# Turning the value product of a sliding-window attention round: V stationary in four column tiles, weights moving, transposes on VectorE

## The chip, the cores and the metric

The kernel runs on one core of one Trainium2 chip. The metric is the device time of one execution in microseconds (us). Before the change it is 310.59 us (median of 3 runs, 309.92 to 311.50).

Engine names: PE is TensorE's matmul, PEld its weight load, DVE is VectorE, ACT ScalarE, POOL GpSimd, SP SyncE. L233 is line 233 of the kernel of the run in question; the same statement has another line number in another kernel. A matmul has a stationary operand (`lhsT`), which a weight load brings into the array (3260 loads for 3200 matmuls in the kernel before), and a moving operand (`rhs`), whose columns the matmul goes through (512 of them every 0.216 us in this kernel). PSUM is the memory that matmuls write.

## The reference, cut to what matters

```python
# x: 2048 tokens x 512; H = 32 heads of 16; window W = 256; F = 1792; all bf16
xn = layernorm(x)
def attention(xn):
    q, k, v = heads(xn @ wqkv)
    s = q @ k.T * 16 ** -0.5
    s = where((i - j >= 0) & (i - j < 256), s, -1e9)
    return merge(softmax(s) @ v) @ wo
def mlp(xn):
    return ((xn @ w_gate) * (xn @ w_up)) @ w_down
return x + attention(xn) + mlp(xn)
```

## The kernel before

Tokens go in four chunks T of 512. A chunk has eight head groups (c, par) of four heads each, and a head group has three steps i, so there are 96 steps. A step computes scores transposed (keys on partitions, queries along the free axis) for up to two key blocks, takes exp on ACT and masks the result P on POOL. The value product for a step comes two steps later (LAG). Between these, PE gets "filler" from one ordered list: projections, gate and up, down, output product.

In PSUM, `S` (128x2048 in float32) has one buffer, the accumulator one, and everything else shares three buffers `M`.

```python
GROUPS = (((-2, 0, 0, 0), (0, 0, 2, 128)),     # key block, first and last query block, column in P
          ((-1, 0, 1, 0), (2, 2, 3, 256)),
          ((1, 1, 3, 0), (3, 3, 3, 384)))
self.ppool = pool("ppool", 5)
self.ps_s = pool("ps_s", 1, space=PSUM); self.ps_a = pool("ps_a", 1, space=PSUM)
self.ps_m = pool("ps_m", 3, space=PSUM)

def scores(self, T, c, par, i):
    S = self.ps_s.tile([128, 4, 512], F32, tag="S", name="S")
    for kb, q0, q1, col in parts:
        for e in range(4):                       # four row tiles: 16 or 32 rows each
            nc.tensor.matmul(S[:, e, col:col + n], lhsT=K[rows, c, ...], rhs=Q[rows, c, ...],
                             tile_position=(32 * e, 0), ...)
    nc.scalar.activation(out=P[:, :, lo:hi], in_=S[:, :, lo:hi], func=ACT.Exp, scale=0.25)
    # ... masks of P on POOL ...

def values(self, T, c, par, i):                  # P is stationary, V moves
    for n, (kb, q, j, e) in enumerate(todo):     # up to 4 (key, query) block pairs x 4 heads
        nc.tensor.matmul(acc[:, q, e, 0:17], lhsT=P[:, e, j:j + 128],
                         rhs=self.V[U][:, v, 8 * c + 2 * e + par, 0:17], ...)
    if i == 2:                                   # column 16 of V is 1: the softmax sum
        nc.vector.reciprocal(out=rz[:], in_=acc[:, :, :, 16])
        nc.vector.tensor_tensor(out=o[:, :, c, :, par, :], in0=acc[:, :, :, 0:16], in1=rz..., op=ALU.mult)

def o_transpose(self, T, c):                     # O: tokens on partitions -> OT: features on partitions
    ps = self.ps_m.tile([128, 4, 128], BF16, tag="M", name="oTp")
    for q in range(4):
        nc.tensor.transpose(ps[:, q, :], self.O[T][:, q, 128 * c:128 * c + 128], self.ident[:])
    nc.vector.tensor_copy(out=self.OT[T][:, c, :], in_=ps...)

# filler: gate, up, projections are pieces of 4 matmuls (128x512), down of 5, 5, 4
for g, s in enumerate(steps):
    fill(-1, g)
    self.scores(*s)
    half = total * (done_w + weight[g] / 2) / sum(weight)
    fill(half, g)
    if g >= LAG:
        self.values(*steps[g - LAG])
        valued = g - LAG
    done_w += weight[g]
    fill(total * done_w / sum(weight), g)
```

The softmax here doesn't subtract the row's maximum and nothing guards it: scores larger than these inputs give would overflow.

Of the kernel before, what the change touches and what calls it, by code (L numbers as in the profile page):

```python
# [7 lines left out]
BF16 = mybir.dt.bfloat16  # L8
F32 = mybir.dt.float32
I32 = mybir.dt.int32  # L10
ACT = mybir.ActivationFunctionType
ALU = mybir.AluOpType
# [10 lines left out]
class Kernel:  # L23
# [24 lines left out]
    def setup(self):  # L48
        nc, const, NT, NF = self.nc, self.const, self.NT, self.NF
        self.x = const.tile([128, NT, 512], BF16, name="x")  # L50
        self.Wqkv = const.tile([128, 4, 1536], BF16, name="Wqkv")
        self.Wo = const.tile([128, 4, 512], BF16, name="Wo")
        self.Wg = const.tile([128, 4, self.F], BF16, name="Wg")
        self.Wu = const.tile([128, 4, self.F], BF16, name="Wu")
        self.Wd = const.tile([128, NF, 512], BF16, name="Wd")
        xv = self.x_d.rearrange("(t p) d -> p t d", p=128)
        wq = self.w_d["qkv"].rearrange("(k p) n -> p k n", p=128)
        wg = self.w_d["g"].rearrange("(k p) n -> p k n", p=128)
        wu = self.w_d["u"].rearrange("(k p) n -> p k n", p=128)
        for t in range(4):  # L60
            nc.sync.dma_start(out=self.x[:, t, :], in_=xv[:, t, :])
        for lo in (1024, 512, 0):
            nc.scalar.dma_start(out=self.Wqkv[:, :, lo:lo + 512], in_=wq[:, :, lo:lo + 512])
        h = self.F // 2
        nc.sync.dma_start(out=self.x[:, 4:8, :], in_=xv[:, 4:8, :])
        for lo in (0, h):
            nc.sync.dma_start(out=self.Wg[:, :, lo:lo + h], in_=wg[:, :, lo:lo + h])
            nc.sync.dma_start(out=self.Wu[:, :, lo:lo + h], in_=wu[:, :, lo:lo + h])
        nc.sync.dma_start(out=self.x[:, 8:NT, :], in_=xv[:, 8:NT, :])
        nc.sync.dma_start(out=self.Wd[:], in_=self.w_d["d"].rearrange("(f p) n -> p f n", p=128))  # L70
        nc.sync.dma_start(out=self.Wo[:], in_=self.w_d["o"].rearrange("(c p) n -> p c n", p=128))

        warm = const.tile([128, 1], F32, name="warm")
        nc.vector.memset(warm[:], 0.0)
        nc.scalar.activation(out=warm[:], in_=warm[:], func=ACT.Exp)
        ident = const.tile([128, 128], BF16, name="ident")
        nc.gpsimd.memset(ident[:], 0.0)
        nc.gpsimd.affine_select(out=ident[:], in_=ident[:], compare_op=ALU.not_equal, fill=1.0,
                                base=0, pattern=[[-1, 128]], channel_multiplier=1)
        self.ident = ident  # L80
        wps = self.ps_a.tile([128, 128], F32, tag="acc", name="wps")
        for _ in range(36):
            nc.tensor.matmul(wps[:], lhsT=ident[:], rhs=ident[:], start=True, stop=True)
        pi = const.tile([128, 1], I32, name="pi")
        nc.gpsimd.iota(pi[:], pattern=[[0, 1]], base=0, channel_multiplier=1)
        podd = const.tile([128, 1], I32, name="podd")
        nc.vector.tensor_scalar(out=podd[:], in0=pi[:], scalar1=4, scalar2=1,
                                op0=ALU.arith_shift_right, op1=ALU.bitwise_and)
        self.odd = const.tile([128, 1], F32, name="odd")
        nc.vector.tensor_copy(out=self.odd[:], in_=podd[:])  # L90
        self.mhalf = const.tile([128, 4], F32, name="mhalf")
        nc.gpsimd.memset(self.mhalf[:], -0.5)
        self.xnT, self.Q, self.hT, self.O, self.OT = {}, {}, {}, {}, {}
        self.K, self.Ko, self.V = {}, {}, {}
        self.strips, self.acc = {}, {}
# [122 lines left out]
                                            fill=0.0, base=0, channel_multiplier=1)  # L218
        self.strips[(T, c, par, i)] = P

    def values(self, T, c, par, i):
        nc = self.nc
        P = self.strips.pop((T, c, par, i))
        if i == 0:
            self.acc[(T, c, par)] = self.ps_a.tile([128, 4, 4, 18], F32, tag="acc", name="acc")
        acc = self.acc[(T, c, par)]
        first = i == 0
        parts = self.parts(T, i)
        todo = [(kb, q, col + 128 * (q - q0), e) for kb, q0, q1, col in parts
                for q in range(q0, q1 + 1) for e in range(4)]  # L230
        for n, (kb, q, j, e) in enumerate(todo):
            U, v = divmod(4 * T + kb, 4)
            nc.tensor.matmul(acc[:, q, e, 0:17], lhsT=P[:, e, j:j + 128],  # L233
                             rhs=self.V[U][:, v, 8 * c + 2 * e + par, 0:17],
                             start=(first and n == 0), stop=(i == 2 and n == len(todo) - 1),
                             skip_group_check=True)
        if i == 2:
            self.acc.pop((T, c, par))
            if (c, par) == (0, 0):
                self.O[T] = self.chunk2.tile([128, 4, 512], BF16, tag="O", name=f"O{T}")  # L240
                self.OT[T] = self.const.tile([128, 4, 512], BF16, tag="OT", name=f"OT{T}")
            rz = self.small.tile([128, 4, 4], F32, tag="rz")
            nc.vector.reciprocal(out=rz[:], in_=acc[:, :, :, 16])  # L243
            o = self.O[T].rearrange("p q (c e two d) -> p q c e two d", c=4, e=4, two=2)
            nc.vector.tensor_tensor(out=o[:, :, c, :, par, :], in0=acc[:, :, :, 0:16],
                                    in1=rz.unsqueeze(3).to_broadcast([128, 4, 4, 16]), op=ALU.mult)

    def o_transpose(self, T, c):
        nc = self.nc
        ps = self.ps_m.tile([128, 4, 128], BF16, tag="M", name="oTp")  # L250
        for q in range(4):
            nc.tensor.transpose(ps[:, q, :], self.O[T][:, q, 128 * c:128 * c + 128], self.ident[:])  # L252
        nc.vector.tensor_copy(out=self.OT[T][:, c, :], in_=ps.rearrange("p q t -> p (q t)"))


    def gate(self, T, f):
# [55 lines left out]
    def fillers(self):  # L312


        out = []
        NCH, NF, NG = self.NCH, self.NF, 24

        def add(cost, f, before=None, after=None):
            out.append((cost, f, before, after))
# [30 lines left out]
            for lo, hi in ((0, 5), (5, 10), (10, NF)):  # L350
                add(hi - lo, lambda lo=lo, hi=hi: self.down(T, b, lo, hi))

        def ot(T, c):
            add(1, lambda: self.o_transpose(T, c), None, NG * T + 6 * c + 5)

        for c in range(1, 4):
            qk(0, c, 6 * c)
        for T in range(NCH):
            if T:
                for c in range(3):  # L360
                    ot(T - 1, c)
                down(T - 1, 0)
                ot(T - 1, 3)
                for b in range(4):
                    if b:
                        down(T - 1, b)
                    add(4, lambda T=T, b=b: self.finish(T - 1, b))
            gu(T, norms(T + 1) if T + 1 < NCH else {})
            if T + 1 < NCH:
                project(T + 1)  # L370
        T = NCH - 1
        down(T, 0)
        for c in range(3):
            ot(T, c)
        for b in range(4):
            if b:
                down(T, b)
            add(3, lambda b=b: self.finish_early(T, b))
        return [(*o, None, None)[:4] for o in out]

    def run(self):
        self.xns, self.stats, self.y0 = {}, {}, {}
        self.setup()
        NCH, NG, LAG = self.NCH, 24, 2
# [12 lines left out]
        nc = self.nc  # L397
# [6 lines left out]
        done_w, spent, n = 0, 0, 0  # L404
        valued = -1

        def fill(upto, group):
            nonlocal spent, n
            while n < len(work):
                cost, f, before, after = work[n]  # L410
                if after is not None and after > valued:
                    break
                if spent + cost / 2 > upto and not any(
                        w[2] is not None and w[2] <= group for w in work[n:]):
                    break
                f()
                spent += cost
                n += 1

        for g, s in enumerate(steps):  # L420
            fill(-1, g)
            self.scores(*s)
            half = total * (done_w + weight[g] / 2) / sum(weight)
            fill(half, g)
            if g >= LAG:
                self.values(*steps[g - LAG])
                valued = g - LAG
            done_w += weight[g]
            fill(total * done_w / sum(weight), g)
        for g in range(len(steps) - LAG, len(steps)):  # L430
            fill(spent + 11, -1)
            self.values(*steps[g])
            valued = g
        fill(10 ** 9, -1)
        assert n == len(work)
        self.o_transpose(NCH - 1, 3)
        for b in range(4):
            self.finish_late(NCH - 1, b)

# [36 lines left out]
```

## Time and profile before

| | before |
|---|---|
| time, median | 310.59 us |
| span of the profiled run | 308.1 us |
| PE busy | 289.0 us, 94% |
| first scores, first scores of chunk 1, last scores | 21.5, 77.2, 291.1 us |

From the page of the kernel before: the line of busy times (share of the span, then instructions), the rows of PE, DVE and granted clock over 40 equal slices in tenths, the chain of waits by engine, and two groups of instructions (busy us, mean ns of one, then idle time before them).

```profile
PE 289.0 (94%) x3200; PEld 144.1 (47%) x3260; DVE 167.2 (54%) x329; ACT 181.6 (59%) x118; POOL 155.3 (50%) x266
...
PE   6569999999999999999999999999999999999992
...
DVE  3237888646531687863722397772842165663324
...
PEclk9999999999999999999999999999999999999999
...
PE 88%; ACT 4%; DMA 3%; issue 2%; DVE 1%; ACTq 0%; DVEq 0%
...
L207 ACT ACTIVATE P<-S 128x2048 bf16<-128x2048 f32 (+2 forms) x96 | 170.0, 1771 | 95.3 <-PE S L199 90.0
...
L233 PEld LDWEIGHTS <-P 128*128 128x128 bf16 x1440 | 49.7, 96 | 21.0 <-issue 0.2
```

PE is the limit. It is busy for 90% or more of every slice from 4 to 39, and the chain that ended last is PE for 88%. The value product needs 1440 loads of a 128-column stationary operand.

The timeline of PE of the kernel before, in chunk 1 (start us, us, engine, line, operation, output<-moving,stationary, shapes, count):

```profile
123.14 0.59 PE L271 MATMUL up<-xnT_754,Wu 128*128 128x512 bf16 x2
123.78 0.35 PE L233 MATMUL acc<-V_164,P 128*128 128x17 bf16 x8
123.99 0.34 PE L233 MATMUL acc<-V_993,P 128*128 128x17 bf16 x8
124.19 0.38 PE L143 MATMUL xTp<-ident,xn 128*128 128x128 bf16 x4
124.41 1.03 PE L262 MATMUL gp<-xnT_754,Wg 128*128 128x512 bf16 x4
125.37 0.29 PE L199 MATMUL S<-Q_990,Ko_163 32*128 32x256 bf16 x4
```

Read starts, not durations: the durations of pipelined matmuls overlap (one of the value matmuls is shown with 170 ns, and the next starts 25 ns after it). Sixteen value matmuls hold PE from 123.78 to 124.19, 25 ns each, for 17 moving columns. Four transposes hold it for 0.22 us.

The waits of PE in the kernel before (total us, times, longest):

```profile
PE S L199 <- ACT P L207: 0.9, 4, 0.4
```

Scores almost never wait for exp to release the one `S` buffer.

### The profile page before, as it was taken

Reading aid. Unit: us, or ns where it says so; the run is one execution under the profiler, and the core shown is the slowest. Engines: PE = TensorE matmul, PEld = TensorE weight load, DVE = VectorE, ACT = ScalarE, POOL = GpSimd, SP = SyncE. Lnnn points to the kernel's source line nnn. Section 1 sums busy time; section 2 is a strip of 40 time slices with the busy share of each in tenths; the row PEclk is TensorE's granted clock in tenths of the full one; section 3 lists DMA queues with packets and bytes.
Section 4 is the critical chain, followed back from the end, with each engine's and each line's share of the span. In section 5 each row is a group of like instructions: output and inputs, shape, how many; then the busy total and the mean of one; then the engine's idle time right before and its main releaser. Section 6 shows DMA issues by size and latency. Waiting matters only on the chain.

```text
span 308.1 us, 7448 instructions
## 1 busy us (share of the span) xinstructions
PE 289.0 (94%) x3200; PEld 144.1 (47%) x3260; DVE 167.2 (54%) x329; ACT 181.6 (59%) x118; POOL 155.3 (50%) x266
## 2 busy tenths in 40 slices
PE   6569999999999999999999999999999999999992
PEld 5334445544544444554544444554454444444550
DVE  3237888646531687863722397772842165663324
ACT  2246666677566576568657565667657566565600
POOL 3115565455555647456555557555455555554520
PEclk9999999999999999999999999999999999999999
DMA  7998000000000000000000000000001000000001
GB/s 238 371 369 284 3 3 1 2 2 0 3 19 34 19 2 0 2 3 0 2 19 19 34 2 3 0 2 2 2 0 37 19 17 3 2 0 2 2 0 68
DMA packets 10512, 12.27 MB, mean 40 GB/s; under 512 B 496, under 2 KB 10480, under 8 KB 10480
## 3 DMA queue, kind: packets, MB, share of 16 engines
q1 hardware_dynamic: 8896, 10.23, 9.8%
q10 hardware_dynamic: 1584, 1.57, 1.6%
q8 instruction: 25, 0.41, 0.6%
q14 instruction: 7, 0.06, 0.1%
HBM read 9.70 MB, written 2.10 MB: 38 GB/s over the span
## 4 chain that ended last, share of the span: by engine, by line
PE 88%; ACT 4%; DMA 3%; issue 2%; DVE 1%; ACTq 0%; DVEq 0%
PE psd L280 16%; PE up L271 16%; PE gp L262 15%; PE acc L233 11%; PE S L199 10%; PE qkp L165 8%; PE psd L285 4%; PE vp L155 4%; ACT P L207 3%; DMA Wqkv<-in_A_wqkv_dram 3%; PE oTp L252 1%; PE xTp L143 1%; PE qkb L181 1%; DMA out_dram<-y 1%; ACT xnT_184 L146 1%
## 5 line engine op out<-in xcount | busy, mean ns | idle before, releaser
L207 ACT ACTIVATE P<-S 128x2048 bf16<-128x2048 f32 (+2 forms) x96 | 170.0, 1771 | 95.3 <-PE S L199 90.0
L212 POOL TENSOR_SCALAR_AFFINE_SELECT P<-P 128x512 bf16<-128x512 bf16 x128 | 81.5, 637 | 70.4 <-ACT P L207 70.2
L216 POOL TENSOR_SCALAR_AFFINE_SELECT P<-P 128x512 bf16<-128x512 bf16 x112 | 71.6, 639 | 56.8 <-ACT P L207 56.8
L233 PEld LDWEIGHTS <-P 128*128 128x128 bf16 x1440 | 49.7, 96 | 21.0 <-issue 0.2
L265 DVE CAST gsb<-gp 128x512 bf16<-128x512 f32 x56 | 38.3, 684 | 13.8 <-PE gp L262 12.6
L271 PEld LDWEIGHTS <-Wu 128*128 128x128 bf16 x224 | 18.2, 97 | 20.7 <-issue 5.0
L262 PEld LDWEIGHTS <-Wg 128*128 128x128 bf16 x224 | 18.4, 97 | 19.7 <-issue 3.9
L243 DVE RECIPROCAL rz<-acc 128x16 f32<-128x16 f32 x32 | 8.0, 251 | 28.8 <-PE acc L233 28.8
L292 DVE TENSOR_TENSOR y<-psd,x 128x512 bf16<-128x512 f32 x12 | 8.3, 691 | 19.7 <-PE psd L285 19.7
L233 PE MATMUL acc<-V_164,P 128*128 128x17 bf16 x384 | 15.6, 170 | 0.2
L233 PE MATMUL acc<-V_993,P 128*128 128x17 bf16 x384 | 15.5, 170 | 0.2
L233 PE MATMUL acc<-V_2172,P 128*128 128x17 bf16 x384 | 15.5, 170 | 0.2
L165 PEld LDWEIGHTS <-Wqkv 128*128 128x128 bf16 x120 | 9.7, 97 | 10.8 <-issue 2.2
L262 PE MATMUL gp<-xnT_1936,Wg 128*128 128x512 bf16 x54 | 14.3, 379 | 0.1
L262 PE MATMUL gp<-xnT_754,Wg 128*128 128x512 bf16 x54 | 14.3, 379 | 0.1
L262 PE MATMUL gp<-xnT_184,Wg 128*128 128x512 bf16 x53 | 14.1, 379 | 0.2
L271 PE MATMUL up<-xnT_184,Wu 128*128 128x512 bf16 x53 | 14.1, 380 | 0.1
L262 PE MATMUL gp<-xnT_3108,Wg 128*128 128x512 bf16 x53 | 14.1, 380 | 0.1
L271 PE MATMUL up<-xnT_3108,Wu 128*128 128x512 bf16 x52 | 13.9, 380 | 0.1
L280 PE MATMUL psd<-Wd,hT_392 128*128 128x512 bf16 x54 | 13.8, 380 | 0.1
L280 PE MATMUL psd<-Wd,hT_1581 128*128 128x512 bf16 x53 | 13.6, 380 | 0.2
L280 PE MATMUL psd<-Wd,hT_2753 128*128 128x512 bf16 x53 | 13.6, 379 | 0.2
(130 smaller groups left out, 378.9 us busy)
## 6 DMA issues: line engine op xcount, KB each, us to landing
out_dram<-y SPq DMA_DIRECT2D x16, 128.0 KB, 1.7
Wg<-in_B_w_gate_dram SPq DMA_DIRECT2D x2, 896.0 KB, 10.0
Wu<-in_B_w_up_dram SPq DMA_DIRECT2D x2, 896.0 KB, 11.4
Wd<-in_B_w_down_dram SPq DMA_DIRECT2D x1, 1792.0 KB, 17.9
Wqkv<-in_A_wqkv_dram ACTq DMA_DIRECT2D x3, 512.0 KB, 6.2
x<-in_A_x_dram SPq DMA_DIRECT2D x1, 1024.0 KB, 15.0
x<-in_A_x_dram SPq DMA_DIRECT2D x4, 128.0 KB, 5.2
x<-in_A_x_dram SPq DMA_DIRECT2D x1, 512.0 KB, 8.2
```

The costliest lines, as they stand in the source:

```text
L155: nc.tensor.matmul(ps[:], lhsT=self.xnT[T][:, k, 128 * b:128 * b + 128], rhs=self.Wqkv[:, k, 1024:1536], start=(k == 0), stop=(k == 3))
L165: nc.tensor.matmul(ps[:], lhsT=self.Wqkv[:, k, lo:lo + 128], rhs=self.xnT[T][:, k, :], start=(k == 0), stop=(k == 3))
L199: nc.tensor.matmul(S[:, e, col:col + n], lhsT=(self.Ko if par else self.K)[U][rows, c, 128 * j:128 * j + 128], rhs=self.Q[T][rows, c, 128 ...
L207: nc.scalar.activation(out=P[:, :, lo:hi], in_=S[:, :, lo:hi], func=ACT.Exp, scale=0.25)
L212: nc.gpsimd.affine_select(out=P[:, :, j:j + 128], in_=P[:, :, j:j + 128], pattern=[[0, 4], [1, 128]], compare_op=ALU.is_ge, fill=0.0, base ...
L216: nc.gpsimd.affine_select(out=P[:, :, j:j + 128], in_=P[:, :, j:j + 128], pattern=[[0, 4], [-1, 128]], compare_op=ALU.is_gt, fill=0.0, bas ...
L233: nc.tensor.matmul(acc[:, q, e, 0:17], lhsT=P[:, e, j:j + 128], rhs=self.V[U][:, v, 8 * c + 2 * e + par, 0:17], start=(first and n == 0), ...
L262: nc.tensor.matmul(ps[:], lhsT=self.Wg[:, k, 128 * f:128 * f + 128], rhs=self.xnT[T][:, k, :], start=(k == 0), stop=(k == 3))
L265: nc.vector.tensor_copy(out=self.gsb[:], in_=ps[:])
L271: nc.tensor.matmul(ps[:], lhsT=self.Wu[:, k, 128 * f:128 * f + 128], rhs=self.xnT[T][:, k, :], start=(k == 0), stop=(k == 3))
L280: nc.tensor.matmul(self.psd[:], lhsT=self.hT[T][:, f, 128 * b:128 * b + 128], rhs=self.Wd[:, f, :], start=(f == 0), stop=False)
L285: self.nc.tensor.matmul(ps[:], lhsT=self.OT[T][:, c, 128 * b:128 * b + 128], rhs=self.Wo[:, c, :], start=first and c == cs[0], stop=(c == ...
```

## The change

Intent: make the small operand stationary. V of one head (128 keys x 17 columns) is loaded into one of four 32-column tiles of the array, the four heads of a group side by side, and P moves with up to 384 columns per matmul. The sums then come out transposed (features on partitions). Two 32x32 block transposes on DVE bring them to the layout that the output product wants: one in float32 before the division, one in bf16 after it. The PE transposes and their PSUM tiles fall away. The value product of all three steps of a head group is issued in one go, right after a scores block.

```diff
-    def values(self, T, c, par, i):
-        ...
-            nc.tensor.matmul(acc[:, q, e, 0:17], lhsT=P[:, e, j:j + 128],
-                             rhs=self.V[U][:, v, 8 * c + 2 * e + par, 0:17], ...)
-        if i == 2:
-            nc.vector.reciprocal(out=rz[:], in_=acc[:, :, :, 16])
-            nc.vector.tensor_tensor(out=o[:, :, c, :, par, :], in0=acc[:, :, :, 0:16], in1=rz..., op=ALU.mult)
-    def o_transpose(self, T, c): ...
+    def values(self, T, c, par):
+        acc = self.accb                       # one accumulator, set to zero once
+        first = True
+        for i in range(3):
+            P = self.strips.pop((T, c, par, i))
+            for kb, q0, q1, col in self.parts(T, i):
+                n, (U, v) = 128 * (q1 - q0 + 1), divmod(4 * T + kb, 4)
+                for e in range(4):
+                    nc.tensor.matmul(acc[32 * e:32 * e + 17, 128 * q0:128 * q0 + n],
+                                     lhsT=self.V[U][:, v, 8 * c + 2 * e + par, 0:17],
+                                     rhs=P[:, e, col:col + n], start=first, stop=(i == 2),
+                                     tile_position=(0, 32 * e), skip_group_check=True)
+                first = False
+        ...
+        nc.vector.transpose(out=at.rearrange("p b r -> p (b r)"), in_=acc[:])
+        nc.vector.reciprocal(out=rz[:], in_=at[:, :, 16])
+        nc.vector.tensor_tensor(out=self.on[:, :, par, :], in0=at[:, :, 0:16], in1=rz..., op=ALU.mult)
+        if par == 1:
+            nc.vector.transpose(out=self.OT[T][:, c, :], in_=self.on.rearrange("p b r d -> p (b r d)"))
@@ run
+        def values(g):
+            if g >= 0 and steps[g][3] == 2:   # only after the third step of a head group
+                self.values(*steps[g][:3]); valued = g
         for g, s in enumerate(steps):
             fill(-1, g)
             self.scores(*s)
-            half = total * (done_w + weight[g] / 2) / sum(weight)
-            fill(half, g)
-            if g >= LAG:
-                self.values(*steps[g - LAG])
-                valued = g - LAG
+            values(g - LAG)
             done_w += weight[g]
             fill(total * done_w / sum(weight), g)
```

Cut: the fillers that called `o_transpose`, the conditions that hold the output product back until its sums exist, and the PSUM tile of the warm-up matmuls.

More of the change, by code (lines that the diff above doesn't have):

```diff
@@ L80, in setup @@
         self.ident = ident
-        wps = self.ps_a.tile([128, 128], F32, tag="acc", name="wps")
+        self.accb = self.ps_a.tile([128, 512], F32, name="accb")
+        nc.vector.memset(self.accb[:], 0.0)
+        wps = self.ps_m.tile([128, 128], F32, tag="M", name="wps")
         for _ in range(36):
@@ L219, in scores @@
         self.strips[(T, c, par, i)] = P
-    def values(self, T, c, par, i):
+    def values(self, T, c, par):
         nc = self.nc
-        P = self.strips.pop((T, c, par, i))
-        if i == 0:
-            self.acc[(T, c, par)] = self.ps_a.tile([128, 4, 4, 18], F32, tag="acc", name="acc")
-        acc = self.acc[(T, c, par)]
-        first = i == 0
-        parts = self.parts(T, i)
-        todo = [(kb, q, col + 128 * (q - q0), e) for kb, q0, q1, col in parts
-                for q in range(q0, q1 + 1) for e in range(4)]
-        for n, (kb, q, j, e) in enumerate(todo):
-            U, v = divmod(4 * T + kb, 4)
-            nc.tensor.matmul(acc[:, q, e, 0:17], lhsT=P[:, e, j:j + 128],
-                             rhs=self.V[U][:, v, 8 * c + 2 * e + par, 0:17],
-                             start=(first and n == 0), stop=(i == 2 and n == len(todo) - 1),
-                             skip_group_check=True)
-        if i == 2:
-            self.acc.pop((T, c, par))
-            if (c, par) == (0, 0):
-                self.O[T] = self.chunk2.tile([128, 4, 512], BF16, tag="O", name=f"O{T}")
-                self.OT[T] = self.const.tile([128, 4, 512], BF16, tag="OT", name=f"OT{T}")
-            rz = self.small.tile([128, 4, 4], F32, tag="rz")
-            nc.vector.reciprocal(out=rz[:], in_=acc[:, :, :, 16])
-            o = self.O[T].rearrange("p q (c e two d) -> p q c e two d", c=4, e=4, two=2)
-            nc.vector.tensor_tensor(out=o[:, :, c, :, par, :], in0=acc[:, :, :, 0:16],
-                                    in1=rz.unsqueeze(3).to_broadcast([128, 4, 4, 16]), op=ALU.mult)
@@ L248, in o_transpose @@
-    def o_transpose(self, T, c):
-        nc = self.nc
-        ps = self.ps_m.tile([128, 4, 128], BF16, tag="M", name="oTp")
-        for q in range(4):
-            nc.tensor.transpose(ps[:, q, :], self.O[T][:, q, 128 * c:128 * c + 128], self.ident[:])
-        nc.vector.tensor_copy(out=self.OT[T][:, c, :], in_=ps.rearrange("p q t -> p (q t)"))
+        acc = self.accb
[10 more added lines that the diff above has]
+                first = False
@@ new lines, in values @@
+        if (c, par) == (0, 0):
+            self.OT[T] = self.chunk2.tile([128, 4, 512], BF16, tag="OT", name=f"OT{T}")
+        if par == 0:
+            self.on = self.work.tile([128, 16, 2, 16], BF16, tag="on", name="on")
+        at = self.work.tile([128, 16, 32], F32, tag="at", name="at")
+        nc.vector.transpose(out=at.rearrange("p b r -> p (b r)"), in_=acc[:])
+        rz = self.small.tile([128, 16], F32, tag="rz")
+        nc.vector.reciprocal(out=rz[:], in_=at[:, :, 16])
+        nc.vector.tensor_tensor(out=self.on[:, :, par, :], in0=at[:, :, 0:16],
+                                in1=rz.unsqueeze(2).to_broadcast([128, 16, 16]), op=ALU.mult)
@@ L256, in gate @@
+        if par == 1:
+            nc.vector.transpose(out=self.OT[T][:, c, :],
+                                in_=self.on.rearrange("p b r d -> p (b r d)"))
     def gate(self, T, f):
@@ L351, in down @@
                 add(hi - lo, lambda lo=lo, hi=hi: self.down(T, b, lo, hi))
-        def ot(T, c):
-            add(1, lambda: self.o_transpose(T, c), None, NG * T + 6 * c + 5)
         for c in range(1, 4):
@@ L359, in fillers @@
             if T:
-                for c in range(3):
-                    ot(T - 1, c)
                 down(T - 1, 0)
-                ot(T - 1, 3)
                 for b in range(4):
@@ L366, in fillers @@
                         down(T - 1, b)
-                    add(4, lambda T=T, b=b: self.finish(T - 1, b))
+                    add(4, lambda T=T, b=b: self.finish(T - 1, b), None, NG * T - 1)
             gu(T, norms(T + 1) if T + 1 < NCH else {})
@@ L372, in fillers @@
         down(T, 0)
-        for c in range(3):
-            ot(T, c)
         for b in range(4):
@@ L377, in fillers @@
                 down(T, b)
-            add(3, lambda b=b: self.finish_early(T, b))
+            add(3, lambda b=b: self.finish_early(T, b), None, NG * T + 17)
         return [(*o, None, None)[:4] for o in out]
@@ L418, in fill @@
                 n += 1
+        def values(g):
+            nonlocal valued
+            if g >= 0 and steps[g][3] == 2:
+                self.values(*steps[g][:3])
+                valued = g
         for g, s in enumerate(steps):
@@ L422, in run @@
             self.scores(*s)
-            half = total * (done_w + weight[g] / 2) / sum(weight)
-            fill(half, g)
-            if g >= LAG:
-                self.values(*steps[g - LAG])
-                valued = g - LAG
+            values(g - LAG)
             done_w += weight[g]
             fill(total * done_w / sum(weight), g)
-        for g in range(len(steps) - LAG, len(steps)):
-            fill(spent + 11, -1)
-            self.values(*steps[g])
-            valued = g
+        fill(spent + 22, -1)
+        values(len(steps) - 1)
         fill(10 ** 9, -1)
         assert n == len(work)
-        self.o_transpose(NCH - 1, 3)
         for b in range(4):
```

## The prediction

> **What bounds it now.** TensorE. The busy table gives PE 94% of the 308.1 us span (ACT 59%, DVE 54%); the chain of waits is 88% PE. From the first scores (21.5 us) to the last (291 us) the timeline shows almost no PE gap. Costs read from it: a 128x512 matmul every 0.216 us; a block of 16 value matmuls 0.40 us, 25 ns each, although each streams only 17 columns [...]; a scores block 0.42 us with the changes of tiling around it. 888 large matmuls outside prologue and tail (about 194 us), 96 scores blocks (41) and 1440 value matmuls (37) make up the observed 270 us.
>
> **What the change removes from PE.** 1440 value matmuls become 704, moving 128 to 384 columns. Per head group, before: 48 x 25 ns = 1.22 us (0.92 in the first chunk). After: 1536 columns (1152), if the four column tiles run together, 0.64 us (0.48) at the trace's rate, plus about 15 ns per set of four as between the sets of a scores block, plus 0.1 us for one more change of tiling: 0.83 us (0.64). 24 x 0.39 + 8 x 0.28 = 11.6 us saved. The 64 output transposes on PE go too: 3.5 us. Together 15 us. The trace shows concurrency for row tiles (four score matmuls start within some 10 ns); for column tiles [...] no run here shows it yet. Serial tiles would cost 2.6 us per group, some 45 us in all.
>
> **What comes back.** (1) The single scores buffer: scores start to exp start 0.54, exp 1.88, release 0.05 = 2.47 us for a full step. A step now holds about 3 us of PE work. After, value work is lumped into every third step; the others hold 0.42 + filler of 8 or 12 matmuls, 2.15 or 3.0 us, and the short ones wait for exp. Counting filler per step with the kernel's own loop gives about 9 us of such waits, against about 1 before. Net on PE: some 7 us.
> (2) DVE. [...] the trace's casts grow 0.40 us from 128 to 512 columns, so I estimate 0.7 us per transpose of either type. Per head group DVE goes from 0.67 us to 0.7 + 0.2 + 0.4, per pair from a 0.42 us copy to a 0.7 us transpose: about +24 us, from 167 to 191. In gate/up stretches with the norms DVE is already about 86% busy; there it becomes nearly full, and evictions will hold the three PSUM buffers: 1 to 3 us lost. Prologue and tail change by under 1 us.
>
> **Prediction: 304 us**, 80% range 291 to 319. Faster by over 2%: 0.50; within 2%: 0.33; slower: 0.17.
>
> **What would show it.** Value matmuls of a set starting within some 10 ns, block about 0.8 us: right; starts spaced by a full stream: wrong. PE busy at about 270 us or below; a new wait of scores on exp of 5 to 12 us, mostly on steps without values. DVE near 190 us, transposes near 0.7 us, DVE slices at 9 in gate/up, and PE gaps there released by DVE casts.
>
> **What would make it wrong.** Column tiles sharing the read of the moving operand (340 or more); a float32 transpose costing double (DVE +22 us, slower or same); tiling changes costing more than 0.1 us; or scores waits hidden better than I count, giving 295.

The sum came to 304 us: 310.6, less 15 us of PE work, plus 8 of added waits for exp, plus 1 to 3 lost to a fuller DVE (worked out so, 304.5 to 306.5). That the four column tiles run together, on which the 0.83 us of a value block and so the 11.6 us rest, was the assumption. The 0.7 us of a transpose, on which the 24 us of DVE rest, was the 0.40 us by which a cast grows from 128 to 512 columns added to a term; no DVE transpose had been measured, but a cast of 128x512 takes 0.68 us in the kernel before, and one of 128x128 0.29 us. The 0.1 us for a change of tiling is the estimate from that kernel's trace, where scores start 0.31 us after the start of the large matmul ahead of them and two large matmuls start 0.216 us apart.

## The result, and the profile after

The changed kernel takes 301.47 us (median of 4 runs, 300.87 to 302.62) against 311.04 us for the kernel before in the same rounds. The ratio is 0.9689 (95% interval 0.9628 to 0.975). Ratios here are the mean time of one kernel's fast runs over that of the other's of the same rounds, so they are not quite the ratio of the medians.

A note on states. Two runs of one experiment below count as slow and are left out, two experiments with a single run have no state, and all other runs count as fast. Among the fast runs of every kernel some have a mean granted clock of 0.98 or less and take up to 4.4 us more. In most of the pages taken in such a run the PEclk row drops to 5 in slices 2 and 3, in the prologue; the pages of runs 1, 3, 5, 6, 11 and 12 below are of this kind, so their prologues are not compared. Where 1% matters I also give "quiet" means, over the runs with a clock of 0.99 or more: 309.9 to 310.1 us for the kernel before in the three sets of rounds below, 301.3 us for the changed one.

From the page of the kernel after, the lines that answer to those above:

```profile
PE 274.7 (92%) x2424; PEld 119.6 (40%) x2460; DVE 194.3 (65%) x362; ACT 181.5 (61%) x118; POOL 156.8 (52%) x266
...
PE   6569989999999999999999999999999999999992
...
DVE  3238898985823599984942489985763357877325
...
PE 68%; ACT 17%; DVE 6%; DMA 3%; issue 3%; POOL 1%; ACTq 1%; DVEq 0%
...
L245 DVE STREAM_TRANSPOSE at<-accb 128x512 f32<-128x512 f32 x32 | 22.9, 715 | 32.6 <-PE accb L234 32.2
...
L234 PE MATMUL accb<-P,V 128*17 128x384 bf16 (+2 forms) x704 | 25.4, 276 | 0.0
...
L234 PEld LDWEIGHTS <-V 128*17 128x17 bf16 x704 | 13.8, 90 | 8.7 <-issue 5.5
```

PE is still the busiest, but ACT has come onto the chain with 17%, and DVE shows runs of 8 and 9 where it had 7 and 8.

The timeline of PE of the kernel after, one scores block and one value block of chunk 1:

```profile
122.75 0.40 PE L201 MATMUL S<-Q,Ko 32*128 32x256 bf16 x8
123.08 0.83 PE L234 MATMUL accb<-P,V 128*17 128x128 bf16 x24
123.85 0.39 PE L261 MATMUL gp<-xnT,Wg 128*128 128x512 bf16 x1
```

A whole head group's value product, 24 matmuls with 4 x 1536 moving columns, holds PE for 0.77 us (123.08 to 123.85). At the 512-column rate of 0.216 us, 1536 columns take 0.65 us and 6144 would take 2.59 us, so the four tiles do stream together; the four matmuls of the first set start within 10 ns (123.082 to 123.092 us).

The waits of PE in the kernel after:

```profile
PE S L201 <- ACT P L209: 6.1, 23, 0.6
...
PE gp L261 <- DVE gsb L264: 0.5, 1, 0.5
```

The view counts only idle time of 0.15 us or more after the modelled end of a matmul, so it counts short. Read from starts, a scores block usually starts 0.31 us after the start of the large matmul ahead of it. Counting each matmul's delay beyond the usual spacing of its kind, from the first to the last scores, the waits for exp are 7.7 us, against 1.0 before, and those for DVE 1.4 us, against 0.6.

To see where the time went I cut PE's matmul records into runs of one kind and counted each run from its first start to the next run's first start. A wait therefore lands in the run ahead of it. So does the time of a large matmul whose record is missing: the value rows hold about 2.3 us of this both before (11 times) and after (10 times), which cancels in the difference. Prologue and tail (0.1 and 0.7 us shorter) are left out.

| us of PE's time | chunk 0, before | after | chunks 1 to 3 up to the last scores, before | after |
|---|---|---|---|---|
| value product | 7.9 | 4.4 | 30.4 | 20.3 |
| transposes (xn, and O before) | 1.1 | 1.6 | 6.3 | 2.3 |
| scores | 6.6 | 6.7 | 23.5 | 23.6 |
| large matmuls and waits behind them | 40.1 | 42.8 | 153.7 | 159.7 |
| stretch | 55.7 | 55.6 | 213.9 | 205.8 |

The value product gave 3.5 + 10.1 = 13.6 us and the transposes 3.5 us. The large matmuls, nearly the same number of them, became 2.7 + 6.0 = 8.7 us slower; most of this is the added waits for exp, 6.7 us. Half of the gain was given back there, and in chunk 0 all of it.

The steps show how. In chunks 1 to 3 the three steps of a head group took 3.17, 2.95 and 2.91 us on average before. After, they take 2.78, 3.21 (the one with the value block) and 2.70 us, and the shortest steps sit at 2.46 us, which is the turn-round of `S`: 0.53 from the start of scores to the start of exp, 1.88 of exp, and 0.05 for the release. Of the 27 scores blocks that clearly waited, 26 follow a step without values.

### The profile page after: what moved, and what is told of

It reads as the page before. It is cut to its first block, busy times and chain, and to the rows that moved or that the text cites. A ratio compares the mean times of both kernels' runs of the same rounds, so it can differ in the third digit from the quotient of the medians.

```text
span 299.1 us, 5877 instructions
## 1 busy us (share of the span) xinstructions
PE 274.7 (92%) x2424; PEld 119.6 (40%) x2460; DVE 194.3 (65%) x362; ACT 181.5 (61%) x118; POOL 156.8 (52%) x266
## 3 DMA queue, kind: packets, MB, share of 16 engines
q1 hardware_dynamic: 8896, 10.23, 10.1%
## 4 chain that ended last, share of the span: by engine, by line
PE 68%; ACT 17%; DVE 6%; DMA 3%; issue 3%; POOL 1%; ACTq 1%; DVEq 0%
ACT P L209 16%; PE psd L279 15%; PE up L270 12%; PE gp L261 11%; PE S L201 10%; PE accb L234 7%; PE qkp L167 6%; DMA Wqkv<-in_A_wqkv_dram 3%; PE vp L157 2%; PE psd L284 2%; DVE at L245 1%; PE xTp L145 1%; DVE hT L272 1%; DVE st L114 1%; PE qkb L183 1%
## 5 line engine op out<-in xcount | busy, mean ns | idle before, releaser
L261 PE MATMUL gp<-xnT,Wg 128*128 128x512 bf16 x213 | 57.1, 380 | 1.4 <-DVE gsb L264 0.5
L270 PE MATMUL up<-xnT,Wu 128*128 128x512 bf16 x216 | 57.3, 380 | 0.5
L279 PE MATMUL psd<-Wd,hT 128*128 128x512 bf16 x213 | 51.7, 380 | 1.4 <-issue 1.3
L272 DVE TENSOR_TENSOR hT<-up,gsb 128x512 bf16<-128x512 f32 x56 | 38.5, 687 | 11.0 <-PE up L270 8.0
L245 DVE STREAM_TRANSPOSE at<-accb 128x512 f32<-128x512 f32 x32 | 22.9, 715 | 32.6 <-PE accb L234 32.2
L279 PEld LDWEIGHTS <-hT 128*128 128x128 bf16 x224 | 19.8, 97 | 25.9 <-issue 5.3
L167 PE MATMUL qkp<-xnT,Wqkv 128*128 128x512 bf16 x117 | 27.5, 380 | 0.5 <-issue 0.5
L234 PE MATMUL accb<-P,V 128*17 128x384 bf16 (+2 forms) x704 | 25.4, 276 | 0.0
L201 PE MATMUL S<-Q,Ko 32*128 32x256 bf16 (+2 forms) x352 | 18.4, 275 | 3.8 <-ACT P L209 3.6
L201 PE MATMUL S<-Q,K 16*128 16x256 bf16 (+2 forms) x352 | 18.4, 275 | 2.6 <-ACT P L209 2.4
L167 PEld LDWEIGHTS <-Wqkv 128*128 128x128 bf16 x120 | 10.7, 98 | 13.7 <-issue 2.5
```

The costliest lines, as they stand in the source:

```text
L167: nc.tensor.matmul(ps[:], lhsT=self.Wqkv[:, k, lo:lo + 128], rhs=self.xnT[T][:, k, :], start=(k == 0), stop=(k == 3))
L201: nc.tensor.matmul(S[:, e, col:col + n], lhsT=(self.Ko if par else self.K)[U][rows, c, 128 * j:128 * j + 128], rhs=self.Q[T][rows, c, 128 ...
L234: nc.tensor.matmul(acc[32 * e:32 * e + 17, 128 * q0:128 * q0 + n], lhsT=self.V[U][:, v, 8 * c + 2 * e + par, 0:17], rhs=P[:, e, col:col + ...
L245: nc.vector.transpose(out=at.rearrange("p b r -> p (b r)"), in_=acc[:])
L261: nc.tensor.matmul(ps[:], lhsT=self.Wg[:, k, 128 * f:128 * f + 128], rhs=self.xnT[T][:, k, :], start=(k == 0), stop=(k == 3))
L270: nc.tensor.matmul(ps[:], lhsT=self.Wu[:, k, 128 * f:128 * f + 128], rhs=self.xnT[T][:, k, :], start=(k == 0), stop=(k == 3))
```

## The experiments

Theory: (a) the column tiles stream together and save what the table shows; (b) the PE transposes were worth their own 3.5 us; (c) half of it returns because the value work is lumped and filler comes in pieces of four, so the short steps wait for exp; (d) DVE, 27 us busier, holds filler back in the gate/up stretches. Rivals: the gain is short weight loads or schedule and not tiling; DVE alone is the new limit; DVE is free.

The diffs below are cut to the lines that matter; left out are mainly the changes to the last steps (runs 3, 7 and 10), the other filler kinds in runs 5 and 6, and the calls that issue the late transpose (run 10).

| run | median us | ratio | quiet mean us |
|---|---|---|---|
| all heads in one column tile (wrong result) | 359.48 (one run) | | |
| value matmuls tile by tile | 320.79 (one run, clock 0.967) | | |
| before, values lumped | 316.83 | 1.0171 (1.0107 to 1.0235) | 316.4 |
| before, no PE transposes of O (wrong) | 306.11 | 0.9835 (0.9782 to 0.9888) | 305.5 |
| before, fine filler | 310.64 | 0.998 (0.9925 to 1.0035) | 308.9 |
| after, fine filler | 299.18 | 0.9613 (0.9564 to 0.9662) | 298.3 |
| after, values spread over the steps | 301.66 | 0.9729 (0.9651 to 0.9807) | 301.5 |
| after, float32 transpose twice | 309.13 | 0.9956 (0.9889 to 1.0024) | 308.9 |
| after, multiply on POOL | 312.39 | 1.0024 (0.9963 to 1.0085) | 311.5 |
| after, multiply on POOL, transpose issued late | 317.77 | 1.0229 (1.0176 to 1.0282) | none quiet |
| the same with fine filler | 307.69 | 0.9904 (0.9862 to 0.9945) | none quiet |
| after, fine filler, norm application on POOL | 307.42 | 0.9873 (0.9822 to 0.9924) | 303.5 (one run) |

### 1. Do the column tiles stream together? Tile by tile

```diff
-        for i in range(3):
-            for kb, q0, q1, col in self.parts(T, i):
-                for e in range(4):
+        for e in range(4):
+            for m, (P, i, kb, q0, q1, col) in enumerate(sets):      # the same six sets
                     nc.tensor.matmul(acc[32 * e:32 * e + 17, ...], ..., tile_position=(0, 32 * e))
```

> The changed kernel with only the order of its value matmuls altered: all sets of one column tile before the next tile, same instructions, same result. My theory (the four column tiles stream at the same time because neighbours in the order sit in different tiles): the tiles now run one after another, a value block takes 2.6 us instead of 0.77, 24 x 1.8 + 8 x 1.4 = 55 us more, about 355 us. Rival (the shorter block comes from the short weight loads, not from tiles running together): the order does not matter, 300 to 304 us.

Correct; 320.79 us in one run, with the disturbed start (first scores at 24.4 us instead of 21.4). The order matters, so the rival that short weight loads alone explain the gain falls. The size was wrong, though. The timeline of PE of this run:

```profile
129.09 0.40 PE L201 MATMUL S<-Q,Ko 32*128 32x256 bf16 x8
129.42 1.51 PE L235 MATMUL accb<-P,V 128*17 128x128 bf16 x24
130.87 0.39 PE L261 MATMUL gp<-xnT,Wg 128*128 128x512 bf16 x1
```

The block takes 1.45 us, not 0.77 and not 2.6. If matmuls started strictly in program order, a tile's first could not start before the sixth of the tile before it, 1408 columns later, and the block would need 3 x 1408 + 1536 columns, 2.4 us by the 512-column rate. So some overlap remained that strict order forbids. The starts of the single matmuls show it. A tile's six matmuls have 128, 384, 256, 256, 384 and 128 columns. The first starts are 129.42 (128 columns), 129.48 (384), 129.65 (256) and 129.65 (128); the fourth of tile 0, which has 256 columns, starts only at 129.75. So tile 1's first matmul, seventh in the program, has started ahead of three of tile 0. By their columns the starts fall into four such chains, which begin at 129.42, 129.65, 129.88 and 130.11 us; all 24 blocks of chunks 1 to 3 show the same order.

In chunk 0 a tile has only four matmuls, and there this order costs almost nothing: at 33.39 us the first matmuls of all four tiles start within 0.04 us, and a block takes 0.63 us against 0.60 in the changed kernel. The 24 larger blocks cost 24 x 0.68 = 16.3 us, and with the disturbed start that is the 20 us. What decides how early a later tile may start was not tested.

The next run asks whether a tile may also stream faster than I counted.

### 2. One column tile

```diff
-                    nc.tensor.matmul(acc[32 * e:32 * e + 17, ...], ..., start=first, tile_position=(0, 32 * e))
+                    nc.tensor.matmul(acc[0:17, ...], ..., start=first and e == 0, tile_position=(0, 0))
-        nc.vector.memset(self.accb[:], 0.0)
+        nc.vector.memset(self.accb[:], 1.0)
```

> The changed kernel with all four heads' value matmuls in column tile 0, in the same order with the same operands; the sums of four heads mix and three quarters of the accumulator keep the ones they are set to at the start, so the result is wrong on purpose. Asks why going tile by tile cost 20 us and not 55. Theory 1 ([...] that run still had two tiles streaming together): with one tile nothing can overlap, a block takes 2.6 to 2.8 us, 350 to 360 us. Theory 2 (a column tile streams faster than I count, about two columns per step of a 128-column matmul): a block takes about 1.4 us, about 320 us.

359.48 us with a quiet clock of 0.997. The timeline of PE:

```profile
131.63 0.40 PE L201 MATMUL S<-Q,K 16*128 16x256 bf16 x8 [0.23 <-ACT P L209]
131.96 2.79 PE L234 MATMUL accb<-P,V 128*17 128x128 bf16 x24
134.68 0.39 PE L270 MATMUL up<-xnT,Wu 128*128 128x512 bf16 x1
```

2.72 us for the block: the same 24 matmuls, columns and weights. Four tiles against one are 2.72 / 0.77 = 3.5 times faster, and on this alone the change would have lost by 49 us instead of winning. A single tile streams no faster than the full array: 2.72 us for 6144 columns, where the 512-column rate gives 2.59 us. The 1.45 us of the run before is then overlap between tiles, as its starts say.

### 3. The schedule alone

```diff
-            fill(half, g)
-            if g >= LAG:
-                self.values(*steps[g - LAG])
+            if g >= LAG and steps[g - LAG][3] == 2:
+                for v in range(g - LAG - 2, g - LAG + 1):
+                    self.values(*steps[v])          # P stationary, as before
```

> The kernel before with the schedule of the changed one: values of three steps in one block right after the scores, filler not halved; the value product and the output transposes on PE as before. My theory: PE work is unchanged, but the steps without values are short and their successor's scores wait for exp; counted from the filler loop about 6 us more, so about 316 us, ratio 1.015 to 1.025, with 5 us or more of scores waits on exp in the waits. Rival (the gain of the change comes from its schedule): 305 us or less.

Ratio 1.0171; quiet mean 316.4 against 309.9 us, 6.5 us more, where 6 was counted. The clock row of its page shows the disturbed start in this profiled run:

```profile
PEclk9559999999999999999999999999999999999997
```

The waits of PE:

```profile
PE S L199 <- ACT P L207: 5.4, 20, 0.6
```

With the old value product, lumping alone raises the waits for exp from 0.9 to 5.4 us. The schedule is a cost of the change, not its gain.

### 4. The PE transposes alone

```diff
-        for q in range(4):
-            nc.tensor.transpose(ps[:, q, :], self.O[T][:, q, 128 * c:128 * c + 128], self.ident[:])
-        nc.vector.tensor_copy(out=self.OT[T][:, c, :], in_=ps...)
+        nc.vector.tensor_copy(out=self.OT[T][:, c, :]..., in_=self.O[T][:, :, 128 * c:128 * c + 128])
```

> The kernel before without the 64 output transposes on PE and their PSUM tiles: DVE copies O to OT untransposed, so the result is wrong on purpose. My theory: 64 x 0.055 us = 3.5 us less, about 307 us, ratio 0.985 to 0.992. Rival (the transposes with their PSUM buffers were the main cost that the change removed): ratio 0.975 or less. Second rival (they were hidden): ratio 1.00.

Ratio 0.9835, just below the expected range; quiet means 309.9 to 305.5 us. In the cut of PE's time over chunks 1 to 3 the transposes fall from 6.3 to 1.8 us, of which about 0.5 us was a wait for DVE. So their price, 4.4 us, is somewhat above the 3.5 us of their PE time, and nearer to it than to either rival. With runs 3 and 4 the value product's own share follows, if effects add: 301.3 - 309.9 = -8.6 = 6.5 - 4.4 + rest, so the rest is -10.7 us, the turned product less what its DVE work costs.

### 5 and 6. Finer filler, in the kernel before and after

In both kernels every piece of four matmuls becomes two pieces of two, and the down product goes in pieces of two. Work and order stay the same.

```diff
-                add(4, lambda f=f: self.gate(T, f))
-                add(4, lambda f=f: self.up(T, f))
+                for ks in ((0, 1), (2, 3)):
+                    add(2, lambda f=f, ks=ks: self.gate(T, f, ks))   # PSUM tile opened at ks 0, evicted after 3
+                for ks in ((0, 1), (2, 3)):
+                    add(2, lambda f=f, ks=ks: self.up(T, f, ks))
```

> The kernel before with its filler cut into pieces of two matmuls instead of four or five; work unchanged. Control for the same cut in the changed kernel. My theory: PE hardly waits for exp here (0.9 us in the waits), so the cut is worth 0 to 1 us: ratio 0.995 to 1.002. Rival (finer filler helps any version equally): ratio 0.985 or less.

> The changed kernel with its filler cut into pieces of two matmuls. My theory (what the change loses again is mostly scores waiting for exp in steps whose filler is 8 matmuls): every step now holds 2.5 us or more, the waits shrink from 9 to 3 us, about 296 us, ratio to before 0.950 to 0.957, PE wait on exp in the waits from 6.1 to under 2.5 us. Rival (DVE holds the filler back): no change, ratio 0.967 to 0.971.

Before: 0.998, as the control should be (quiet 309.9 to 308.9 us). After: 0.9613, quiet mean 301.3 to 298.3 us. That is real but about half of what I expected. The waits of PE in the changed kernel with fine filler:

```profile
PE gp L271 <- DVE hT L288: 1.3, 3, 1.0
...
PE S L209 <- ACT P L217: 1.0, 4, 0.4
PE gp L271 <- DVE gsb L276: 0.9, 3, 0.5
```

The wait for exp fell from 6.1 to 1.0 us, as the theory says, and waits for DVE came up from 0.8 to 2.2 us before gate matmuls. Counted from starts, waits for exp fall from 7.7 to 1.8 us and waits for DVE rise from 1.4 to 3.8: 3.5 us net, and the stretch from the first to the last scores is 3.4 us shorter (261.4 to 258.0). (The rows of the cut mislead here: the value product rises from 20.3 to 21.6 us only because more matmul records behind it are missing, 15 against 9; the block itself still takes 0.77 us.) So (c) is shown for the larger part, and the rest went to (d). This version is the fastest.

### 7. Values spread over the steps

```diff
-            if g >= 0 and steps[g][3] == 2:
-                self.values(*steps[g][:3])
+            if g >= 0:
+                self.values(*steps[g])        # the two sets of this step only, column tiles kept
```

> The changed kernel with the values of each step issued in their own step again (column tiles kept): filler steps even out, but the tiling changes two more times per head group, and the first value block of a group comes one step after the last block of the group before, so it may wait for the DVE transpose of the one accumulator. My theory: waits for exp from 9 to 3 us, extra changes of tiling 3.5 us, so 298 to 301 us if the accumulator is free in time, and new PE waits on the DVE transpose if it is not. Rival (lumping costs nothing): 304 us or more.

301.66 us, quiet 301.5 against 301.3: nothing changed. From the waits of PE:

```profile
PE S L201 <- ACT P L209: 1.1, 4, 0.4
...
PE accb L233 <- DVE at L246: 0.3, 1, 0.3
```

The steps became even (3.01, 2.78, 2.90 us) and the wait for exp fell to 1.1 us. But the value product in chunks 1 to 3 rose from 20.3 to 24.9 us, since it changes the tiling three times per head group instead of once (three blocks of 0.33 us instead of one of 0.77). That is 4.6 us over 24 groups, about 0.1 us for each of the two further changes; the expected 3.5 us was the estimate, and what else the two further blocks may cost was not separated. It took just what the waits gave (159.7 to 155.3 us for the large matmuls). The accumulator was no problem: PE waits once for the transpose, 0.3 us. Lumping saves these 4.6 us and pays with waits for exp.

### 8. Twice the float32 transpose

```diff
         nc.vector.transpose(out=at.rearrange("p b r -> p (b r)"), in_=acc[:])
+        nc.vector.transpose(out=at2.rearrange("p b r -> p (b r)"), in_=at.rearrange("p b r -> p (b r)"))
```

> The changed kernel with each of the 32 float32 transposes followed by a second, useless one into a scratch tile: about 23 us more on DVE. My theory (DVE is full only in the gate/up stretches with norms, about half of its time): about 6 us more, 305 to 310 us, with PE gaps released by DVE casts in the first chunk. Rival (DVE is off the critical path): at most 1 us more, 301 to 302.5 us. Second rival (DVE is the limit throughout): 20 us more.

309.13 us, quiet 308.9: 7.6 us more for 22.8 us more of DVE. DVE is neither free nor the limit throughout. The waits of PE:

```profile
PE S L201 <- ACT P L209: 5.3, 19, 0.6
PE gp L263 <- DVE hT L274: 3.1, 4, 1.5
...
PE gp L263 <- DVE gsb L266: 1.5, 3, 0.5
```

A head group takes 0.26, 0.29 and 0.29 us more in chunks 0, 1 and 2, where gate/up runs beside the norms of the next chunk, and only 0.08 us more in chunk 3, which has no norms beside it. That is theory (d), and it shows where DVE is short.

### 9. The multiply on POOL

```diff
-        nc.vector.tensor_tensor(out=self.on[:, :, par, :], in0=at[:, :, 0:16], ...)
+        nc.gpsimd.tensor_tensor(out=self.on[:, :, par, :], in0=at[:, :, 0:16], ...)
```

> The changed kernel with the multiply by the reciprocal on POOL instead of DVE: 13.7 us less on DVE, 15 to 25 us more on POOL, which was 52% busy. My theory (DVE costs 1 to 3 us in gate/up): 1 to 2 us less, ratio to before 0.962 to 0.967. Rival (DVE off the path): 0.969 or more. If POOL's queue delays the masks of P, value blocks wait for POOL and the time rises.

Quiet mean 311.5 us, 10 us worse; two of its six runs were slow. I had looked at POOL's queue for the danger and not at DVE's. The longest new wait of the run, and what PE waits for DVE, from its waits:

```profile
DVE OT L251 <- POOL on L248: 29.8, 16, 2.7
...
PE gp L261 <- DVE hT L272: 5.9, 4, 2.1
...
PE vp L157 <- DVE hT L272: 2.7, 2, 1.4
```

The timeline of DVE at one such place:

```profile
155.42 0.25 DVE L247 RECIPROCAL rz<-at 128x16 f32<-128x16 f32 x1
157.78 0.71 DVE L251 STREAM_TRANSPOSE OT<-on 128x512 bf16<-128x512 bf16 x1 [2.10 <-POOL on L248]
```

The timeline of POOL at the same place:

```profile
155.93 0.64 POOL L218 TENSOR_SCALAR_AFFINE_SELECT P<-P 128x512 bf16<-128x512 bf16 x1 [1.07 <-ACT P L209]
156.52 0.64 POOL L214 TENSOR_SCALAR_AFFINE_SELECT P<-P 128x512 bf16<-128x512 bf16 x1
157.12 0.62 POOL L248 TENSOR_TENSOR on<-at,rz 128x256 bf16<-128x256 f32 x1
```

POOL takes the multiply in its turn, behind the masks that are already in its queue. DVE's next instruction is the transpose that reads the result, so DVE stands still, 2.1 us here and 1.9 us on average over 16 times, and the evictions behind it with it: PE's waits for `hT` rise from 0.3 to 8.6 us, most of the 10 us lost.

### 10 and 11. The same with the transpose issued later: confounded

```diff
-        if par == 1:
-            nc.vector.transpose(out=self.OT[T][:, c, :], in_=self.on...)
+        if par == 1:
+            self.late = (self.OT[T][:, c, :], self.on)     # issued at the next head group's values
-                    add(4, lambda T=T, b=b: self.finish(T - 1, b), None, NG * T - 1)
+                    add(4, lambda T=T, b=b: self.finish(T - 1, b), None, NG * T + 2)
```

> As the run with the multiply on POOL, but the bfloat16 transpose that reads its result is issued on DVE only at the next head group's values, some 8 us later. Theory (that run lost 10 us because DVE, in order, stood at this transpose until POOL had finished): the DVE wait on POOL falls from 29.8 us to under 2, and the time to 298 to 301 us, ratio 0.957 to 0.970. Rival (POOL itself, by delaying the masks, costs the 10 us): still 308 us or more.

> Fine filler and the late POOL multiply together. Theory (fine filler took away the waits for exp and left about 2 us of waits for DVE after the value blocks): 13.7 us less DVE work takes these too, 295.5 to 297.5 us, ratio 0.951 to 0.958. Rival (what is left is PE work alone): as fine filler alone, ratio 0.960 to 0.963.

317.77 and 307.69 us, so both theories failed. The first rival's number came true (308 us or more), but the trace shows another reason than late masks. The second edit, needed so that the output product does not read before the late transpose, stops the ordered filler list at each chunk's start for more than a step. The timeline of PE of run 10 at the start of chunk 2:

```profile
157.09 1.04 PE L285 MATMUL psd<-Wd,hT 128*128 128x512 bf16 x4
159.22 0.40 PE L201 MATMUL S<-Q,Ko 32*128 32x128 bf16 x8 [1.09 <-ACT P L209]
161.67 0.62 PE L201 MATMUL S<-Q,Ko 32*128 32x256 bf16 x8 [2.06 <-ACT P L209]
162.22 1.46 PE L234 MATMUL accb<-P,V 128*17 128x128 bf16 x24
```

PE has no filler between these scores blocks, and then its matmuls themselves run slowly: the value block takes nearly twice its time (1.46 us, where the view shows 0.83 in the changed kernel), and the granted clock in the window from 150 to 165 us is 0.84. Only chunk 0, which has no output product to hold back, can be read. There a head group takes 6.78 us against 6.95 in the changed kernel, and 6.49 against 6.81 with fine filler. DVE relief does help there. DVE's wait for POOL fell from 29.8 to 7.8 us, not to under 2. What the late transpose is worth over the whole kernel stays open.

### 12. The norm application on POOL

```diff
-        nc.vector.tensor_scalar(out=xn[:], in0=self.x[:, t, :], scalar1=mv..., scalar2=rs..., ...)
+        eng = nc.vector if t < 4 else nc.gpsimd
+        eng.tensor_scalar(out=xn[:], in0=self.x[:, t, :], scalar1=mv..., scalar2=rs..., ...)
```

> Fine filler, and the 12 norm applications after the first chunk on POOL instead of DVE: about 6 us less DVE work, all of it in the gate/up stretches, and no DVE instruction waits for the result. Theory (DVE is short only in these stretches): 1 to 2 us less than fine filler alone, ratio 0.955 to 0.960. Rival: no difference; or, if POOL takes over 1 us for each, late masks and more time.

307.42 us; 303.5 in its one quiet run, against 298.3 for fine filler alone. The group of these instructions:

```profile
L134 POOL TENSOR_SCALAR xn<-x,mv,rs 128x512 bf16<-128x512 bf16 x12 | 24.9, 2078 | 0.0
```

On POOL one takes 2.08 us, where DVE takes 0.44 in the changed kernel. Masks queue up behind it (ACT's waits for masks are 14.5 us, against 11.4 with fine filler alone), but PE waits for a mask only once, 0.2 us. What PE waits for is the result itself: its transposes wait 5.5 us for POOL, about the 5.2 us lost. The expectation named the case (over 1 us for each, more time) but looked at DVE and the masks, not at the PE transposes that read the result.

## Why the prediction was right

It was 304 us with a range of 291 to 319; measured 301.47 us. The range would also have held the time before, so the total alone shows little. Term by term:

- **The value product on PE.** Predicted 11.6 us saved, measured 13.6. The block was put at 0.83 us and takes 0.77. That the four tiles stream together was the assumption; the runs show 3.5 times for four (0.77 against 2.72 us, run 2).
- **The PE transposes.** Predicted 3.5 us; measured 3.5 in the cut of PE's time, and 4.4 when taken away alone (run 4).
- **Waits for exp.** Predicted 9 us against 1; the waits view shows 6.1 against 0.9 (7.7 against 1.0 counted from starts), 26 of 27 after steps without values, and fine filler cuts the view's figure to 1.0 (runs 3, 5 and 6). Their cause is the lumped value work and the coarse filler, as predicted. Spreading the values also removes them, but the value product then takes 4.6 us more (run 7).
- **DVE.** Predicted 191 us and 0.7 us per transpose of either type; measured 194.3, 0.715 and 0.711. The cost is of the predicted kind and place (run 8). DVE is 87 to 89% busy in the gate/up stretches with norms (28 to 68, 105 to 138 and 175 to 208 us), against 75 to 81% before, where the prediction put 86%. The size of the loss, 1 to 3 us, was not measured by itself: run 8 gives 0.33 us of time per us of DVE added, and says nothing certain of the 27 us added before.
- **Misses.** PE busy was to fall to 270 us or below and is 274.7. The PE waits for DVE are only 0.8 us in the view, 1.4 from starts, in the changed kernel; the shortage shows once DVE is loaded more or PE waits less for exp. The final time is better than predicted because the turned value product saves 2 us more than counted and the added waits for exp are 6.7 us instead of 8.

In sum: 13.6 + 3.5 us came off PE, 8.7 us came back around the large matmuls, mostly as waits, and prologue and tail gave 0.8 us. That is the 9 us between the two profiled spans, to within rounding.

## What to carry to other kernels

When a matmul's stationary operand is wide and its moving one narrow, turn it round and put several small stationary operands side by side in column tiles (here 48 matmuls of 25 ns, 1.2 us, became 24 in 0.77 us), but order the instructions so that neighbours sit in different tiles: the same 24 matmuls took 0.77 us so, 1.45 us tile by tile and 2.72 us in one tile (with only four matmuls per tile, going tile by tile cost 0.03 us). Then look at what the faster engine now waits for: with one buffer between two engines, a step cannot be shorter than the buffer's turn-round (2.46 us for `S` here), so cut the other work into pieces small enough to fill each step evenly. Before moving an instruction to an idle engine, see what stands behind its reader in the reader's own queue (in run 9 DVE stood 1.9 us on average, 16 times, behind an instruction moved to POOL).
